# A talking-heads attention and SoLU kernel: new due times in its planner, v in six pieces, a longer ring, another tile order

## Chip, cores and metric

The kernel runs on one core of one Trainium2 chip (trn2). The metric is the device time in microseconds (us) of one execution; three executions of the kernel before gave a median of 728.68 us.

## What is computed

Four batches, 12 heads, 448 positions, 64 values per head; then 1792 tokens (4 x 448) of width 768 through a SoLU layer with 1024 hidden units. All inputs and the output are float32 in their values. Shortened from the reference:

```python
scores = np.matmul(q, k.transpose(0, 1, 3, 2)) / np.sqrt(64)     # q, k, v: (4, 12, 448, 64)
scores = np.einsum('bhij,hg->bgij', scores, w_pre)               # heads mixed before softmax
attn = np.exp(scores - np.max(scores, axis=-1, keepdims=True))
attn = attn / (np.sum(attn, axis=-1, keepdims=True) + 1e-09)
attn = np.einsum('bhij,hg->bgij', attn, w_post)                  # and after it
x = np.matmul(attn, v).transpose(0, 2, 1, 3).reshape(1792, 768)
h = x @ w_in                                                     # 768 x 1024
e = np.exp(h - np.max(h, axis=-1, keepdims=True))
solu = h * e / (np.sum(e, axis=-1, keepdims=True) + 1e-09)
mu = np.mean(solu, axis=-1, keepdims=True)
var = np.mean((solu - mu) ** 2, axis=-1, keepdims=True)
out = ((solu - mu) / np.sqrt(var + 1e-06) * g_ln) @ w_out        # 1024 x 768
```

## The kernel before

Every matmul whose operands are split runs as three float16 products (high x high, high x low, low x high). The attention part walks through the batches b = 0 to 3. Each batch has 45 units u of 10 query rows (the last unit of a batch has 8), gathered in four blocks of 12 or 9 units (120 or 88 rows). Two units make a pair, and one pair passes through these steps, each a task of the planner:

- `qk` (L502, PE), once for two heads and a block: the scores of the block, into PSUM; `sh` (L514, ACT) and `sl` (L519, DVE) write them as high and low halves into a tile `s`, of which there are two.
- `f` (L553, L557, a DMA issued on SP): it gathers 10 rows of all heads from `s` into `sr`, of which there are four.
- `m` (L570, PE): mixing with w_pre. `mx` (L580, DVE) row maximum, `ex` (L596, ACT) exponential with its sum, `gd` and `iv` (L607, L611, DVE) reciprocal of the sum, `w` (L617, POOL) the weights of w_post divided by the sum, `o` (L625, PE) mixing with w_post, `po` (L251 through `copy`, ACT) into the ring `p_t`, 18 units long.
- once per block `av` (L675, PE), six calls of two heads each, then `xh` (L242, ACT) and `xl` (L247, DVE), which write x into `x_t` in two groups of three calls. They share one PSUM bank.

While batch b - 1 runs, q, k and v of batch b are prepared: loads `ld` (issued on POOL), absolute maxima `am` (L405 on DVE for q and k, L403 on ACT for v), a short chain of scales `sc`, the halves `hi` (L244, POOL) and `lo` (L247 on DVE or L437 and L438 on POOL), and DMA transposes `t` (issued on SP). v lies in a pool of two whole tiles of 12 heads, loaded by six transfers; its maxima are taken in four pieces of 768 columns. In the last batch w_in takes the place of the next batch: `fw` (fetch), `wi` (steps that turn 64-bit floats into 32-bit ones), `wm` (L800, maximum), `wh` and `wl` (halves); then `h0`, the hidden matmuls of the first token tile. The x of batches 0 to 2 is stored to DRAM (`xd`), and `x0` loads batch 0's back during the last batch.

The order of all this is fixed when the program is made, by the class `Plan`: a list scheduler with a cost for each task. It keeps for each engine the time at which it is free and takes, again and again, an engine's best task: of those that could start within `LOOK` us of the earliest, the one with the smallest sum of its due time and `RUSH` times its extra wait. With `RUSH = 12.0` and `LOOK = 0.25` that is nearly the one that is ready first; due times come from `at`, `T0 + STEP * (45 b + u)` with T0 = 24 and STEP = 2.25 us. A transfer counts as landed 2.2 us (2.6 us from POOL) plus its bytes after its issue. `ring`, `until` and `more` say how many buffers a tile has and which tasks free them. On the chip each engine then runs its own queue in that order and waits on semaphores.

After the attention part its pools are closed and the SoLU part (`moe`) begins, in plain program order: two pieces of w_out are fetched (`cv_wo`), then x of batches 1 and 2 (`x_fetch`, L729 and L731, on SP). A loop over t then runs `solu_mean(t)`, from t = 11 on `project(t - 11)` (L1397, PE), `hidden(t + 1)` (L838, PE), `solu_head(t + 1)`, `ln(t)`, for t below 8 a conversion of one piece of w_out (L757 to L776), and the DMA transposes `turn`. Tile t is 128 tokens. Pools that are opened here lie on the addresses of those that were closed, so that a first transfer into them waits for the old tile's last reader.

## Time and profile before

| | us |
|---|---|
| median of 3 runs | 728.68 (726.76 to 728.98) |
| the profiled execution | 729.22 |
| its span, first to last instruction | 727.5 |
| PE busy | 642.6 (88%) |
| DVE busy | 506.5 (70%) |
| ACT busy | 454.8 (63%) |
| POOL busy | 271.1 (37%) |
| mean granted clock of PE | 0.97 |

Shares of the whole span mix three parts: a start of some 50 us, the attention part until 492.7 us, when the last x is written, and the SoLU part. They have to be read by stretches: for each stretch the time in which PE did nothing, the clock that it was granted (1.00 is 2.4 GHz, 0.50 is 1.2 GHz), and which other engine was busy nearly all the time. The profiled execution lies 0.5 us above the median of the runs.

### The profile page before, as it was taken

What the parts mean: (1) busy time and instruction counts of PE and PEld (TensorE: products, weight loads), DVE (VectorE), ACT (ScalarE), POOL (GpSimd) and SP (SyncE); (2) the same over time, 40 slices, a digit from 0 to 9 for tenths busy, and PEclk for the clock granted to TensorE, in tenths of its full rate; (3) what the DMA queues carried; (4) which work ended last, traced back from release to release, by engine and by line L of the source; (5) the groups of instructions that cost most, each with busy time, mean ns of one, the idle gap of its engine ahead of it and who ended that gap; (6) DMA issues with size and microseconds to landing.
All of it is one profiled execution on the core that took longest, in us unless ns stands there. A gap on an engine that the chain in (4) does not pass through costs nothing.

```text
span 727.5 us, 17255 instructions
## 1 busy us (share of the span) xinstructions
PE 642.6 (88%) x6418; PEld 427.1 (59%) x6418; DVE 506.5 (70%) x1345; ACT 454.8 (63%) x960; POOL 271.1 (37%) x418
## 2 busy tenths in 40 slices
PE   2677979999899899889998988979998848999997
PEld 2444757777667577667776766754443424566664
DVE  7875998879997569997779999748888764200000
ACT  2655778887688778769798876724555554321111
POOL 3503584124961124871113443502666633320000
PEclk9698999999999999999999998999999979999999
DMA  8037479355678547598266545226367313244112
GB/s 228 14 74 202 128 195 184 126 171 170 201 188 167 126 115 219 189 209 205 79 216 199 198 171 166 59 88 194 91 132 170 59 29 52 51 102 93 44 44 66
DMA packets 114028, 98.51 MB, mean 135 GB/s; under 512 B 69604, under 2 KB 104600, under 8 KB 113944
## 3 DMA queue, kind: packets, MB, share of 16 engines
q1 hardware_dynamic: 108120, 83.62, 43.7%
q0 software_dynamic: 4416, 12.40, 5.9%
q10 hardware_dynamic: 1408, 1.38, 0.7%
q8 instruction: 51, 0.84, 0.5%
q14 instruction: 33, 0.27, 0.1%
HBM read 33.24 MB, written 9.63 MB: 59 GB/s over the span
## 4 chain that ended last, share of the span: by engine, by line
PE 46%; DVE 30%; DMA 8%; ACT 6%; POOL 5%; issue 3%; SPq 1%; ACTq 0%; POOLq 0%; DVEq 0%
PE y L1397 14%; PE po L625 13%; PE px L675 6%; DVE dead L580 5%; PE pm L570 5%; PE ps L502 5%; DVE s L519 4%; DMA sr<-s 4%; PE ps_h L838 3%; POOL wo L776 2%; DVE cv_wo L773 2%; ACT e L596 2%; DVE hl_q L247 2%; DMA raw_q<-in_q_dram 2%; DVE cv_wo L768 1%
## 5 line engine op out<-in xcount | busy, mean ns | idle before, releaser
L625 PE MATMUL po<-wr,e 128*112 128x120 f32 x1440 | 179.3, 278 | 19.6 <-POOL wr L617 19.4
L625 PEld LDWEIGHTS po<-wr,e 128*112 128x112 f32 x1440 | 160.0, 182 | 48.2 <-POOL wr L617 34.7
L617 POOL TENSOR_SCALAR wr<-wq,sm 128x120 f32<-128x120 f32 x180 | 72.9, 415 | 259.2 <-DVE sm L611 92.2
L596 ACT ACTIVATE e<-pm,nb,c_exp 128x448 f32<-128x448 f32 x180 | 132.9, 738 | 31.6 <-DVE dead L580 28.4
L580 DVE TENSOR_SCALAR_CACHE_REDUCE dead<-pm,c_nexp 128x448 f16<-128x448 f32 x180 | 121.8, 677 | 24.4 <-PE pm L570 16.0
L514 ACT ACTIVATE s<-ps 120x448 f16<-120x448 f32 (+1 forms) x192 | 100.1, 549 | 51.8 <-PE ps L502 39.7
L519 DVE SCALAR_TENSOR_TENSOR s<-ps,s 120x448 f16<-120x448 f32 (+1 forms) x192 | 115.5, 617 | 21.6 <-ACT s L514 16.8
L251 ACT COPY p_t<-po 112x480 f32<-112x480 f32 x180 | 109.9, 626 | 16.8 <-PE po L625 16.1
L675 PE MATMUL px<-p_t,raw_v 112*64 112x120 f32 (+1 forms) x1536 | 90.0, 264 | 5.6 <-ACT p_t L251 2.3
L502 PE MATMUL ps<-k,q 64*64 64x448 f16 (+2 forms) x1008 | 82.7, 362 | 11.5 <-DVE s L519 7.1
L838 PE MATMUL ps_h<-wi,xf 128*128 128x512 f16 x396 | 86.8, 379 | 5.7 <-DVE u L1340 5.7
L675 PEld LDWEIGHTS px<-p_t,raw_v 112*64 112x64 f32 x1536 | 74.1, 136 | 26.5 <-issue 15.0
L1397 PE MATMUL y<-wo_h,lth 128*128 128x384 f16 (+2 forms) x224 | 72.7, 331 | 9.8 <-ACT wo_h L242 9.8
L1397 PE MATMUL y<-wo_l,lth 128*128 128x384 f16 (+2 forms) x224 | 72.4, 329 | 2.5 <-DVE wo_l L247 2.0
L1397 PE MATMUL y<-wo_h,ltl 128*128 128x384 f16 (+2 forms) x224 | 72.4, 330 | 0.0
L1397 PEld LDWEIGHTS <-lth 128*128 128x128 f16 x448 | 44.3, 99 | 43.8 <-issue 15.4
L838 PEld LDWEIGHTS <-xf 128*128 128x128 f16 x396 | 38.5, 98 | 52.8 <-issue 7.4
L570 PE MATMUL pm<-sr,wp_hi 64*64 64x448 f16 (+1 forms) x720 | 58.0, 367 | 9.3 <-DMA sr<-s 6.0
L1405 ACT ACTIVATE o<-y,c_out 128x384 f32<-128x384 f32 (+2 forms) x28 | 16.1, 578 | 72.3 <-PE y L1397 72.3
L502 PEld LDWEIGHTS <-q 64*64 64x64 f16 (+2 forms) x1008 | 33.8, 108 | 40.9 <-issue 21.0
L596 ACT ACTIVATION_READ_ACCUMULATOR e<-pm,nb,c_exp 128x1 f32 x180 | 38.4, 213 | 0.0
L570 PE MATMUL pm<-sr,wp_lo 64*64 64x448 f16 (+1 forms) x360 | 36.5, 355 | 0.0
(178 smaller groups left out, 798.8 us busy)
## 6 DMA issues: line engine op xcount, KB each, us to landing
sr<-s SPq DMA_DIRECT2D x176, 210.0 KB
cv_wi<-in_moe_w_in_dram SPq DMA_DIRECT2D x24, 256.0 KB
cv_wo<-in_moe_w_out_dram SPq DMA_DIRECT2D x8, 768.0 KB
raw_k<-in_k_dram POOLq DMA_DIRECT2D x18, 224.0 KB, 4.0
raw_q<-in_q_dram POOLq DMA_DIRECT2D x18, 224.0 KB, 5.6
raw_v<-in_v_dram POOLq DMA_DIRECT2D x18, 224.0 KB, 4.5
xh<-xsh SPq DMA_DIRECT2D x9, 224.0 KB
xl<-xsl SPq DMA_DIRECT2D x9, 224.0 KB
```

The lines of the kernel that those rows point to most:

```text
L251: nc.scalar.copy(out=out, in_=in_)
L502: nc.tensor.matmul(sps[b, c, h + e][lo:hi], q2[b, g][rows, 2 * j + x, i0 + lo : i0 + hi], k1[b, g][rows, 2 * j + y], start=(a == 0), stop= ...
L514: nc.scalar.activation(out=s_t[b, c][0 : y.shape[0], h, 0], in_=y, func=AF.Copy, scale=2.0**-E_S)
L519: nc.vector.scalar_tensor_tensor(out=t[:, h, 1], in0=y, scalar=2.0**-E_S, in1=t[:, h, 0], op0=ALU.mult, op1=ALU.subtract)
L570: nc.tensor.matmul(pmx[b, u + i][64 * e : 64 * e + 64, 0:S], w[rows], sr[b, u][rows, e, z], start=(a == 0), stop=(a == 2),)
L580: nc.vector.tensor_scalar(out=dead, in0=pmx[b, u][:, 0:S], scalar1=c_nexp[0:UK, b : b + 1], scalar2=None, op0=ALU.mult, op1=ALU.min, accum ...
L596: nc.scalar.activation(out=ee[b, u], in_=pmx.pop((b, u))[:, 0:S], func=AF.Exp, bias=nbs.pop((b, u)), scale=c_exp[0:UK, b : b + 1], accum_o ...
L617: ENG[eng].tensor_scalar(out=w, in0=wq[0:UK, 0 : H * UN], scalar1=sm, scalar2=1.0, op0=ALU.mult, op1=ALU.mult)
L625: nc.tensor.matmul(ps[:, c * 120 : (c + 1) * 120], e[:, c * CP : (c + 1) * CP], w, start=True, stop=True)
L675: nc.tensor.matmul(xps[b, blk, g][e * 64 : e * 64 + 64, i, 0:n], raws["v", b][:, h, c * D : (c + 1) * D], block_view(b, blk, c * H + h), s ...
L838: nc.tensor.matmul(ps[:, n], xx[:, kc, o : o + 128], ww[:, kc, n * 512 : (n + 1) * 512], start=(kc == 0 and a == 0), stop=(kc == KDM - 1 a ...
L1397: nc.tensor.matmul(y, xx[:, kc], ww[:, kc, cut], start=(kc == 0 and a == 0), stop=(kc == KFF - 1 and a == 2),)
```

## The change

The planner: `LAG` adds a time by the kind of the transfer to the planned landing (fetch `f` 1 us, `ld` 4.24, `t` 3, `xd` 7.9, `fw` 10). `RUSH` falls from 12.0 to 0.04 and `LOOK` to 0.143, so that of the tasks that are ready within 0.143 us the one due first is taken, nearly whatever it waits. Due times are rewritten: pairs replace units as their clock, 4.2 us for a pair (`PER`), and `AIM` adds an offset to each kind of task, from -182 (`t` of k) to +258 us (`lo` of q); such offsets are ranks more than times. `ld` of k and q become due from the batch's start (`ago(0.6 * i)`), with the same dependence on the `m` of the batch before.

v: its pool has seven tiles of two heads; a piece of the next batch needs the slot that `av` of the last block frees for the same heads. Its maxima are taken in six pieces of 512 columns, each after its own load. The ring `p_t` has 24 units instead of 18, and starts at 15 instead of 9.

SoLU: tiles are taken in the order 11, 12, 13, 0, ..., 10. `x0` is gone; x of batch 0 is fetched with the others after the attention part. `h0` waits for the `xl` of the last batch's first two blocks instead. `wm` may run on ACT. `av` of batch 0 waits for the warming matmuls.

```diff
-    RUSH = 12.0
-    LOOK = 0.25
+    RUSH = 0.04
+    LOOK = 0.143
+    AIM = {
+        "am_k": 211, "am_q": 63, "am_v": 143, "av0": 53, "av1": 46, "av2": 15, "av3": 21, "av4": 63,
+        "av5": -125, "es": 199, "ex0": -9, "ex1": 38, "f0": -126, "f1": -104, "gd0": -94, "h0": 123,
+        "iv0": -15, "ld_v": 45, "lo_k": 140, "lo_q": 258, "lo_q0": 233, "m0": -20, "mix": -100, "mx0": 17,
+        "mx1": 17, "o0": 11, "po0": -10, "qk": -17, "sc_k": -53, "sc_q": -51, "sc_wi": -44, "sh0": -33,
+        "sh1": -168, "sl1": 12, "t_k": -182, "t_q0": -144, "wh": 82, "wi": 93, "wl": 45, "xh0": -26,
+        "xh1": -59, "xl0": -166,
+    }
+    LAG = {
+        "f": 1, "fw": 10, "ld": 4.24, "t": 3, "xd": 7.9,
+    }
...
+        tasks = {k: t[:3] + (t[3] + self.aim(k),) + t[4:] for k, t in self.tasks.items()}
...
+                lag = (2.6 if e == "pool" else 2.2) + self.LAG.get(k[0], 0.0)
...
-                    rings[i] = max(rings[i], t + (2.6 if e == "pool" else 2.2)) + kb / ways / rate
+                    rings[i] = max(rings[i], t + lag) + kb / ways / rate
...
-    T0, STEP = 24, 2.25
-    RING = 18
+    T0, PER = 24, 4.2
+    RING, NV = 24, 7
...
-    v_p = ctx.enter_context(tc.tile_pool(name="vp", bufs=2))
+    v_p = st.enter_context(tc.tile_pool(name="vp", bufs=NV))
...
-        return (RING // 2 + b * NU + u) % RING * UN
+        return (15 + b * NU + u) % RING * UN
...
-        assert n == 2 * m
-        (pp, np), (ce, _) = x.ap
-        return bass.AP(x.tensor, x.offset + i * ce, [[pp, np], [-i * ce, 2], [ce, m]])
+        if n == 2 * m:
+            (pp, np), (ce, _) = x.ap
+            return [(slice(0, n), bass.AP(x.tensor, x.offset + i * ce, [[pp, np], [-i * ce, 2], [ce, m]]))]
+        views = [(slice(0, m), x[:, i : i + m])]
+        return views + ([(slice(m, n), x[:, 0 : n - m])] if m < n else [])
...
-        for i in (i,):
+        for cut in [cut for cut, _ in block_views(b, blk, 0)]:
             for c in range(NCH):
                 for e in range(2):
...
-                        due=at(b - 1, 6 + i) if b else i + 4 * (n == "q"),
+                        due=ago(0.6 * i + 3 * (n == "q")) if b else i + 4 * (n == "q"),
...
-                    after=[("m", b - 1, 14 + 2 * i)] if b else [("am", "q", 0, 1)],
+                    after=[("m", b - 1, 40)] if b else [("am", "q", 0, 1)],
...
-                    until=[("av", b, NBLK[b] - 1, NPAIR - 1)],
+                    until=[("av", b, NBLK[b] - 1, i)],
...
-                    AMV,
+                    {"act": (0.61, 0.71)},
...
-                    after=[("lo", "q", o, NPAIR - 1), ("m", o, i + 4 * kc)],
+                    after=[("lo", "q", o, NPAIR - 1)],
...
-            add(("wm", kc), with_eng(w_in_max, kc), {"dve": 1.13}, after=[prev], due=due + 9)
+            add(("wm", kc), with_eng(w_in_max, kc), {"dve": 1.13, "act": (1.0, 1.1)}, after=[prev], due=due + 12)
...
+    T3 = -(-(B - 1) * S // 128)
+    TURNS = list(range(T3, NT)) + list(range(T3))
...
-        for b, pool, tag in ((1, v_p, "v"), (2, wt_p, "x2")):
+        for b in range(B - 1):
             for i in range(XP):
-                x_fetch(b, i, pool, tag)
+                x_fetch(b, i, wt_p)
```

## Rows read from the trace of the kernel before

**Rows 1.** The page: busy time of PE, and the chain that ended last, by engine

```profile
PE 642.6 (88%) x6418; PEld 427.1 (59%) x6418; DVE 506.5 (70%) x1345; ACT 454.8 (63%) x960; POOL 271.1 (37%) x418
PE 46%; DVE 30%; DMA 8%; ACT 6%; POOL 5%; issue 3%; SPq 1%; ACTq 0%; POOLq 0%; DVEq 0%
```

**Rows 2.** Windows: stretch, its length, busy us by engine, granted clock, DMA share, GB/s

```profile
52.00:72.00 20.00, 13.96 (x133) 8.87 (x133) 11.38 (x33) 11.85 (x29) 6.75 (x13) 0.87 0.70 196
84.00:110.00 26.00, 21.34 (x291) 15.99 (x288) 24.78 (x76) 20.32 (x49) 21.51 (x38) 1.00 0.53 148
110.00:180.00 70.00, 67.56 (x921) 52.05 (x921) 57.95 (x171) 60.26 (x141) 22.70 (x50) 1.00 0.58 158
180.00:220.00 40.00, 35.70 (x439) 26.07 (x437) 37.94 (x111) 31.80 (x73) 30.86 (x55) 1.00 0.71 201
240.00:258.00 18.00, 15.08 (x161) 9.79 (x160) 10.45 (x32) 12.88 (x31) 2.13 (x6) 0.91 0.49 119
286.00:321.00 35.00, 30.38 (x395) 22.41 (x391) 33.36 (x97) 25.81 (x62) 26.81 (x46) 0.95 0.75 210
386.00:452.00 66.00, 57.72 (x702) 41.74 (x695) 64.21 (x147) 53.03 (x116) 26.51 (x33) 0.98 0.59 194
452.00:492.70 40.70, 36.16 (x384) 27.00 (x383) 24.76 (x61) 19.32 (x41) 11.98 (x15) 0.95 0.27 80
492.70:574.90 82.20, 76.46 (x354) 34.30 (x351) 71.57 (x150) 43.31 (x66) 49.28 (x31) 1.00 0.59 136
606.70:727.50 120.80, 117.12 (x698) 68.01 (x695) 10.44 (x32) 26.12 (x42) 14.74 (x11) 1.00 0.30 68
```

**Rows 3.** Chain that ended last, in order of time, near the first batch's start

```profile
56.39 10.51 DMA sr<-s
```

**Rows 4.** Timeline of POOL: first loads of the next batch's k (twelve of k, q)

```profile
54.53 2.04 POOL L393 DMA_DIRECT2D raw_k<-in_k_dram  x3
```

**Rows 5.** Groups by line: count, busy us, mean ns; preparation of q, k, w_in on DVE

```profile
L405 DVE TENSOR_REDUCE am_q<-raw_q 112x1 f32<-112x768 f32 x16 | 15.1, 943 | 1.8 <-DMA raw_q<-in_q_dram 1.8
L247 DVE SCALAR_TENSOR_TENSOR hl_q<-raw_q,p_q,hl_q 112x256 f16<-112x256 f32 x34 | 20.5, 648 | 0.0
L800 DVE TENSOR_REDUCE am_wi<-wi 128x1 f32<-128x1024 f32 x6 | 7.3, 1210 | 0.4 <-POOL wi L776 0.4
```

**Rows 6.** Groups by line: ACT's maxima of v, and its pass over 512 columns

```profile
L403 ACT ACTIVATE ja_v<-raw_v 112x768 f16<-112x768 f32 x16 | 13.9, 871 | 0.0
L242 ACT ACTIVATE hl_q<-raw_q,p_q 112x512 f16<-112x512 f32 x6 | 3.9, 711 | 0.0
L403 ACT ACTIVATION_READ_ACCUMULATOR ja_v<-raw_v 112x1 f32 x16 | 3.6, 225 | 0.0
```

**Rows 7.** Chain that ended last: the low halves of w_in

```profile
469.38 7.63 DVE wi L247 x5
```

**Rows 8.** Groups by line and form, 484 to 492 us: `av` of the last block

```profile
L675 PE MATMUL px<-p_t,raw_v 112*64 112x88 f32 x96 | 4.1, 241 | 2.3 <-DVE xsl L247 1.7 <-ACT p_t L251 0.6
L675 PEld LDWEIGHTS px<-p_t,raw_v 112*64 112x64 f32 x96 | 3.8, 137 | 2.6 <-issue 1.9 <-ACT p_t L251 0.8
```

**Rows 9.** Timeline of SP's queue: fetches of w_out and x

```profile
484.78 0.82 SPq L742 DMA_DIRECT2D cv_wo<-in_moe_w_out_dram  x2
491.12 1.47 SPq L729 DMA_DIRECT2D xf<-xh  x3
501.70 0.60 SPq L731 DMA_DIRECT2D xf<-xsl  x1
505.66 10.01 SPq L742 DMA_DIRECT2D cv_wo<-in_moe_w_out_dram  x2
```

**Rows 10.** The page's DMA issues: count and KB of each piece of x of batch 0

```profile
xf<-xh SPq DMA_DIRECT2D x3, 256.0 KB
```

**Rows 11.** Window with the fetches at full share, and DVE's timeline

```profile
496.00:498.00 2.00, 2.00 (x11) 0.94 (x10) 0.64 (x4) 1.43 (x3) 0.00 (x0) 1.00 1.00 300
511.27 0.55 DVE L757 TENSOR_SCALAR cv_wo<-cv_wo 128x768 uint32<-128x768 uint32 x1
```

More of the change, by code (lines that the diff above doesn't have):

```diff
@@ L39, in add, with aim @@
         self.tasks[key] = (run, on, list(after), due, ring, slots, dma, list(behind), shape)
+    def aim(self, k):
+        if not isinstance(k, tuple):
+            return self.AIM.get("misc", 0.0)
+        n = k[0]
+        if n in ("m", "mx", "ex", "w", "o", "po", "f", "gd", "iv"):
+            n += str(int("pe" not in self.tasks[("m",) + k[1:]][1]))
+        elif n in ("sh", "sl"):
+            n += str(k[3] % 2) + ("p" if k[1] == 0 and k[2] == 0 else "")
+        elif n in ("av", "xh", "xl"):
+            n += str(k[3])
+        elif n in ("hi", "lo", "am", "ld", "t", "tp"):
+            n += "_" + k[1] + ("0" if n == "tp" or k[2] == 0 else "")
+        elif n == "sc":
+            n += "_" + str(k[1])
+        return self.AIM.get(n, 0.0)
     def order(self):
-        tasks, done, out = self.tasks, {}, []
+        done, out = {}, []
+        tasks = {k: t[:3] + (t[3] + self.aim(k),) + t[4:] for k, t in self.tasks.items()}
         held = {r: [] for r in self.size}
@@ L849, in add_tasks, with pt, at @@
         with_eng = lambda f, *a: lambda e: f(*a, e)
-        at = lambda b, u: T0 + STEP * (b * NU + u)
-        none = ()
+        pairs, first = [], {}
+        for b in range(B):
+            for c in range(NBLK[b]):
+                first[b, c] = len(pairs)
+                pairs += [(b, u) for u in range(BLK0[b][c], BLK0[b][c + 1], 2)]
+            first[b, NBLK[b]] = len(pairs)
+        clock = [T0]
+        for b, u in pairs:
+            clock.append(clock[-1] + PER * (1.0 if pair_of(b, u)[1] == 2 else 0.6))
+        when = {g: t for g, t in zip(pairs, clock)}
+        def pt(i):
+            if i != int(i):
+                return pt(i // 1) + PER * (i % 1)
+            i = int(i)
+            if i < 0:
+                return T0 + PER * i
+            return clock[i] if i < len(clock) else clock[-1] + PER * (i - len(clock) + 1)
+        def at(b, u):
+            if u >= NU:
+                return at(b + 1, u - NU) if b + 1 < B else pt(len(pairs)) + PER / 2 * (u - NU)
+            if u < 0 or b < 0:
+                return at(b - 1, u + NU) if b > 0 else T0 + PER / 2 * (b * NU + u)
+            u0, _ = pair_of(b, u)
+            return when[b, u0] + PER / 2 * (u - u0)
         add("mixl", mix_load, {"pool": (2.3, 9.3)}, due=0.0)
@@ L949, in add_tasks @@
                     )
-            add(("es", b), one(exp_scales, b), {"dve": 0.28}, after=es, due=at(b - 1, 35) if b else T0 - -2)
+            add(("es", b), one(exp_scales, b), {"dve": 0.28}, after=es, due=ago(20) if b else T0 - -2)
             for i in range(NPAIR):
@@ L1140, in add_tasks @@
         o = B - 1
-        for i in range(XP):
-            add(
-                ("x0", i),
-                one(x_fetch, 0, i, v_p, "v"),
-                {"sp": 0.57},
-                dma=(16, 229, 18.5),
-                after=[("xd", b, j) for b in range(2) for j in range(XP)] + [("m", o, 28 + 2 * i)],
-                behind=[("x0", i - 1)] if i else [],
-                due=at(o, 30 + 2 * i),
-                ring=None if i else "v",
-                until=["end"],
-            )
         for kc in range(KDM):
-            due = at(o, 18 + 4 * kc)
+            due = pt(first[o, 0] - 3 + 3.2 * kc)
             for i in range(4):
@@ L1193, in add_tasks @@
             )
-            add(("wl", kc), with_eng(w_in_lo, kc), {"dve": 1.19}, after=[("wh", kc)], due=at(o, 33 + 2 * kc))
+            add(("wl", kc), with_eng(w_in_lo, kc), {"dve": 1.19}, after=[("wh", kc)], due=pt(first[o, 0] + 18.5 + 0.8 * kc))
         prev = []
```

141 lines of the change are left out of this document (73 added, 68 removed).

## The prediction, made before the changed kernel was run

> **What bounds the kernel now.** I read the page first, then windows by stage, then inside each weak stage the chain and the timelines. The page says that PE is busy 88% of the span and carries 46% of the chain that ended last, DVE 30% [rows 1]. Such shares mix stages, so the windows come next [rows 2]. In the middle of a batch (110 to 180 us) PE works 67.56 of 70 us: it is the bound there, and 3.5% idle is what the present planner reaches when nothing disturbs. The weak stretches are others, and their idle PE time is the length less the busy time in [rows 2]: 6.0 us in 52 to 72; 4.7 in 84 to 110, 4.3 in 180 to 220 and 4.6 in 286 to 321; 2.9 in 240 to 258; 8.3 in 386 to 452; 4.5 in 452 to 492.7. Together 35.4 us. In five of these the granted clock, 2.4 GHz at 1.00, was also below that, part of the time at 1.2 GHz, in stretches in which PE had idled; the length times the missing share times PE's busy share is what that cost: 1.8, 1.5 (286 to 321), 1.4 (240 to 258), 1.1 and 1.8 us, 7.6 in all. Had these 245.7 us only 3.5% of idle time, 8.6 us would stay. So everything that a better order can win before 492.7 us is 35.4 + 7.6 - 8.6 = 34.4 us.
>
> Behind 492.7 us the loop of the SoLU part is led by DVE (71.57 of 82.2 us), then PE works 117.12 of 120.8 us [rows 2]. The change leaves the work of both as it is; that part moves with the time at which it begins. The time before 52 us I count at nothing: the loads and scales of batch 0 are the same.
>
> **Part by part: due times, RUSH, LOOK, AIM.** These remove no instruction; they change which of two ready tasks is issued first. Before, ready first was issued first, so preparation ran when its data came. The three stretches at 84, 180 and 286 us show it: DVE is busy 24.78 of 26, 37.94 of 40 and 33.36 of 35 us there, but only 57.95 of 70 in 110 to 180 [rows 2]. What fills it is the next batch's maxima and low halves, 0.943 and 0.648 us each (16 and 34 of q, about as many of k) [rows 5], and the softmax of the current pair stands behind them. With offsets of +63 to +258 these become filler for idle moments. The room is there (12 us in 110 to 180), the need is some 18 us for a batch: 8 maxima of 0.943 and about 14 low halves of 0.648, as batch 0 takes 24 of the 66, and scales. The three stretches hold 13.6 us idle and 1.5 of clock, less 3.5% of 101 us: 11.6. I take 60%, 7.0 us, because most of the need fits the room; bounds 0 and 11.6.
>
> The last batch is the same case with w_in: DVE is busy 64.21 of 66 us in 386 to 452 [rows 2]. `fw` no longer waits for a unit of the last batch, and `wm`, 6 of 1.21 us [rows 5], may run on ACT, which has 13 us to spare there. Open: 8.3 + 1.1 - 2.3 = 7.1 us; I take 60%, 4.3. Behind it five low halves of w_in hold DVE for 7.63 us [rows 7] while the last pairs wait. Open in 452 to 492.7: 4.5 + 1.8 - 1.4 = 4.9; I take 40%, 2.0, since all w_in must still be done before `h0`.
>
> **LAG.** It makes no transfer shorter. At the first batch's start one gather into `sr` is in the chain for 10.51 us [rows 3]; POOL had begun to issue the twelve loads of the next k and q at 54.53 us [rows 4], and the sixteen engines moved 196 GB/s in the stretch [rows 2]. Those loads hang on the same `m` as before, so the crowd comes again; the planner can only put other work, a `qk`, ahead of the premix. Open: 6.0 + 1.8 - 0.7 = 7.1; I take a quarter, 1.8. At 240 to 258 it is the transposes and a gather; `t` of k now goes first on SP. Open: 2.9 + 1.4 - 0.6 = 3.7; half, 1.8.
>
> The Trainium skill says the same against this part (DMA: Bandwidth & Descriptors, "Issuing engines are not separate DMA queues"): DMAs from any engine run on the same 16 DMA engines and interleave. The 10.51 us agree, and by that rule alone the 1.8 us would be nothing.
>
> Gain: 7.0 + 4.3 + 2.0 + 1.8 + 1.8 = 16.9 us, with 0 and 34.4 as bounds.
>
> **v in six pieces.** ACT's maxima become 24 of (0.711 + 0.225) us instead of 16 of (0.871 + 0.225) [rows 6]: 22.5 against 17.5 us, 5.0 more. They hide in ACT's idle time, some 10 us of 70 even in the best stretch [rows 2]; without it they would cost 5.0. The loads are as many, but now wait for the slot that `av` of the last block frees, some 5 pairs into the batch. If they are late, POOL stands at the load, and behind it on POOL `w`, and on PE `o`. The first block's `av` needs them only when its own 9 or 12 units are done, and 24 units of ring are more than two blocks; I count nothing.
>
> **Ring of 24.** Starting at 15 + 45b, only one block wraps at a point that isn't its middle: the last block of the last batch starts at (15 + 135 + 36) mod 24 = 18 with 88 rows, 60 before the end and 28 after. Its matmuls become 96 for each group of three calls. Nothing hides them, as the SoLU loop waits for that x. Now 96 matmuls take 4.1 us and their loads 3.8, so 39.6 ns a load [rows 8]. If the loads set the pace, a group takes 96 x 39.6 ns = 3.8 instead of 2.04 us, 1.76 more, 3.5 for both. If time goes by columns, it is 0. The row's loads were themselves paced by matmuls of 42.5 ns, so I take 1.0 a group: 2.0 us.
>
> The Trainium skill (TensorE: Matmul & The Clock Gate, "LDWEIGHTS") gives columns / 1.2 ns, so an estimate of 53 ns for 64 columns; one after the other, 96 would take 5.1 us and both groups lose 6.2. The row's 39.6 ns show that two overlap, so the measurement decides.
>
> **Tile order.** PE's work is the same. Tiles 12 and 13 need no fetch. But `x0` leaves the last batch, and six transfers of 256 KB [rows 10] join the fetches behind it. SP issued eighteen between 491.12 and 502.3 us and the third piece of w_out at 505.66 [rows 9]; six more at half a microsecond still end by 505.7, so it is the bytes that count. DVE takes that piece at 511.27 us [rows 11], 5.6 us after its issue, and its own 786 KB (128 x 768 values of 8 bytes) need 2.6 us at the 300 GB/s of a full window [rows 11]: 3.0 us to spare. The six bring 1.57 MB, 5.2 us at that rate. And the tiles of w_out may now lie on the ring's addresses, so that their first fetches, issued at 484.78 us [rows 9], would wait for `av` until 491.1; the later of them adds 2.6 us there. Queued ahead in full, DVE's loop stands 5.2 + 2.6 - 3.0 = 4.8 us; at best 0. I take 1.0, since the eighteen (2.7 MB by their shapes) filled only 240 of the 300 GB/s over their 11.2 us and leave room for 0.7 MB.
>
> **Sum.** -16.9 + 2.0 + 1.0 = -13.9 us. The profiled execution took 729.22 us, 1.7 of it around its span of 727.5; 729.2 - 13.9 = 715.3 us. The median of the runs lies 0.5 below that execution, so 714.8.
>
> **Rivals.**
> First, the preparation starves. This is the case on the slower side. With ranks of +140 to +258, `am` and `lo` run only when nothing else is ready. The point from which it decides: if less than the 18 us of a batch's need fits into DVE's idle moments before the boundary, the rest stands before `t` and `qk` of the next batch with PE empty. About 13 us fit by [rows 2] (12 in 110 to 180, 1 in 84 to 110), so 5, and with late data 10 us, stay at each of three boundaries. These take the place of 4.5 us idle now: 3 x 5.5 = 16.5, plus 3.0 of costs: 748 us. Against it: units overlap over the boundary, and 220 to 240 and 258 to 286 gave room as well.
> Second, transfers stay the limit. The bursts at 52 and 240 us don't shrink, and w_in is as late as before because its tiles come free no earlier. Then only the three stretches win: 728.7 - 7.0 + 3.0 = 724.7 us.
> Third, the order doesn't do what it says: waits on the chip differ from the planned ones, idle time only moves to other tasks, and the costs remain: 727 to 733 us.
> Fourth, it does all it can: two thirds to nine tenths of the 34.4 us, less 3: 700.7 to 708.7.
>
> **How the numbers follow.** My forecast (709 to 721 us) 0.42; the fourth case and better 0.22; the second (721 to 726.5) 0.14; the third 0.11, about two thirds of it within 0.3% of 728.7; the first 0.11. A measurement of this kernel can tell some 0.3%, 2.2 us, from no change. Faster: 0.42 + 0.22 + 0.13 = 0.77; same 0.09; slower 0.14. The range of 8 in 10 goes from 698 (below it 0.07: the upper bound of the gain and no cost is 694) to 732 (above it 0.13).
>
> **What would show it.** Right: the stretches at a batch's change keep PE idle under 6%, DVE's load is level over a batch, maxima and low halves are scattered; the last x is written near 478 us, and from there to the end it takes some 235 us as before, plus 1. Wrong: a run of `lo` with PE empty before each boundary (first rival); gathers of 10 us again (second); waits of PE as long as before at other lines (third); DVE idle before L757 in the third turn of the SoLU loop (the fetch term); the last block's groups longer or shorter than 3 us (the ring term).

## The result and the profile after

The changed kernel took 722.77 us (median of 4 runs, 721.44 to 723.45) against 728.83 us of the kernel before beside it on the same chip: a ratio of 0.9919, with a 95% interval of 0.9894 to 0.9944. It is faster by some 6 us where 13.9 were forecast. The profiled execution took 722.47 us, its span 720.8; before these were 729.22 and 727.5, so the two profiles differ by 6.75 us.

The page of the changed kernel, busy time by engine and the chain that ended last [rows 1]:

```profile
PE 651.8 (90%) x6514; PEld 430.3 (60%) x6514; DVE 500.4 (69%) x1331; ACT 455.2 (63%) x977; POOL 282.7 (39%) x447
PE 49%; DVE 26%; DMA 8%; ACT 6%; issue 5%; POOL 4%; SPq 2%; POOLq 0%; DVEq 0%; ACTq 0%
```

The last x of the attention tells the two halves of the kernel apart. DVE's timelines have its last piece here, in the kernel before and in the changed one:

```profile
491.79 0.87 DVE L247 SCALAR_TENSOR_TENSOR xsl<-px,x_sc,xsh 128x80 f16<-128x80 f32 x4 [2.89 <-ACT xsh L242]
476.52 0.87 DVE L276 SCALAR_TENSOR_TENSOR xsl<-px,x_sc,xsh 128x80 f16<-128x80 f32 x4 [3.89 <-ACT xsh L271]
```

It ends at 492.66 us before and at 477.39 after: the attention won 15.3 us (forecast: -16.9 + 2.0 = -14.9). From there to the end of the span it took 243.4 us, before 234.8: the SoLU part lost 8.6 us (forecast: 1.0). Gain and loss make the 6.7 us. So the question is where the 8.6 us came from, and whether the 15.3 were won for the reasons that I gave.

**The attention by stage**, the windows of [rows 2], in the changed kernel (the first row, 20 to 52 us, is new):

```profile
20.00:52.00 32.00, 25.86 (x246) 15.44 (x243) 27.81 (x66) 20.40 (x45) 12.05 (x19) 0.89 0.23 58
52.00:72.00 20.00, 16.26 (x192) 11.01 (x189) 14.52 (x38) 14.59 (x33) 9.14 (x18) 1.00 0.72 194
84.00:110.00 26.00, 24.31 (x286) 17.64 (x286) 25.49 (x72) 21.68 (x51) 21.57 (x41) 1.00 0.62 167
110.00:180.00 70.00, 69.64 (x914) 52.25 (x916) 59.08 (x171) 62.33 (x148) 29.23 (x61) 1.00 0.62 183
180.00:220.00 40.00, 35.70 (x426) 26.43 (x424) 34.11 (x102) 30.44 (x73) 22.30 (x40) 1.00 0.78 175
240.00:258.00 18.00, 17.92 (x231) 13.09 (x233) 14.29 (x41) 16.57 (x39) 7.36 (x15) 1.00 0.58 155
286.00:321.00 35.00, 30.23 (x384) 23.13 (x382) 30.81 (x98) 28.21 (x71) 22.61 (x43) 0.95 0.93 209
386.00:452.00 66.00, 60.03 (x698) 44.97 (x690) 59.52 (x147) 53.70 (x119) 27.81 (x34) 0.97 0.44 138
```

and the kernel before in that first stretch:

```profile
20.00:52.00 32.00, 22.43 (x218) 13.98 (x216) 25.77 (x61) 18.50 (x37) 8.63 (x18) 0.79 0.16 38
```

PE is busier by 3.4 us in 20 to 52, 2.3 in 52 to 72, 3.0 in 84 to 110, 2.1 in 110 to 180, 2.8 in 240 to 258 and 2.3 in 386 to 452, and no busier in 180 to 220 and 286 to 321. From the second batch on the windows no longer hold the same work, since the changed kernel runs ahead. ACT's copies into `p_t` show by how much. There are 180, 45 for each batch; the 45th, 90th, 135th and 180th end at about 160, 271, 373 and 485 us before and at 152, 251, 363 and 468 after, so 9, 20, 10 and 17 us ahead.

**The SoLU part.** Its loop is followed by the start of each product `u` (L1340 before, L1401 after), counted from the last x, in us:

```
turn              0     1     2     3     4     5     6     7     8     9     10     11     12    end of span
before         6.55 14.91 24.66 34.39 44.13 53.88 63.62 73.36 80.81 87.32 102.23 114.03 125.08  234.84
after          7.73 16.07 29.32 39.40 49.47 59.53 69.60 79.67 86.24 92.74 107.67 119.47 133.07  243.41
later by       1.18  1.16  4.66  5.01  5.34  5.65  5.98  6.31  5.43  5.42   5.44   5.44   7.99    8.57
```

Four steps are seen: 1.2 us before the first turn, 3.5 in turn 2, some 0.33 in each of the five turns behind it (10.07 us instead of 9.74; 0.9 of it comes back in turn 8), and 2.55 between turns 11 and 12. SP's timeline shows what stands ahead of turn 2:

```profile
475.95 0.81 SPq L775 DMA_DIRECT2D cv_wo<-in_moe_w_out_dram  x2
477.48 3.74 SPq L762 DMA_DIRECT2D xf<-xh  x3
481.27 2.73 SPq L762 DMA_DIRECT2D xf<-xl  x3
495.17 0.61 SPq L764 DMA_DIRECT2D xf<-xsl  x1
495.88 9.85 SPq L775 DMA_DIRECT2D cv_wo<-in_moe_w_out_dram  x2
```

The 24 transfers of x are issued from 477.48 to 495.8 us: 18.3 us, and up to 1.78 us for one. The third piece of w_out goes out behind them at 495.88, though ACT's maximum, which reads its buffer last, was done at 491.5:

```profile
491.29 0.19 ACT L1351 ACTIVATION_READ_ACCUMULATOR cv_wo<-wo 128x1 f32 x1
```

In DVE's timeline the piece is taken with a wait of 4.08 us (the next ones with half a microsecond to one, and a longer instruction; their rows are in the last section):

```profile
501.32 0.56 DVE L790 TENSOR_SCALAR cv_wo<-cv_wo 128x768 uint32<-128x768 uint32 x1 [4.08 <-DMA cv_wo<-in_moe_w_out_dram]
```

The chain that ended last goes through a fetch in each of these turns, which it did in none before:

```profile
495.88 5.34 DMA cv_wo<-in_moe_w_out_dram
505.38 4.64 DMA cv_wo<-in_moe_w_out_dram
515.46 5.11 DMA cv_wo<-in_moe_w_out_dram
```

### The profile page after: what moved, and what is told of

It is laid out like the page before. It is cut to its first block, busy times and chain, and to the rows that moved or that the text cites. A ratio compares the mean times of both kernels' runs of the same rounds, so it can differ in the third digit from the quotient of the medians.

```text
span 720.8 us, 17481 instructions
## 1 busy us (share of the span) xinstructions
PE 651.8 (90%) x6514; PEld 430.3 (60%) x6514; DVE 500.4 (69%) x1331; ACT 455.2 (63%) x977; POOL 282.7 (39%) x447
## 4 chain that ended last, share of the span: by engine, by line
PE 49%; DVE 26%; DMA 8%; ACT 6%; issue 5%; POOL 4%; SPq 2%; POOLq 0%; DVEq 0%; ACTq 0%
PE y L1458 15%; PE po L659 14%; PE px L708 6%; PE pm L604 5%; PE ps L534 5%; DVE dead L614 5%; DVE s L551 4%; DMA cv_wo<-in_moe_w_out_dram 4%; PE ps_h L876 3%; DMA sr<-s 2%; ACT e L630 2%; DVE hl_k L276 2%; DVE sm L641 2%; DVE hl_q L276 1%; DVE u L1387 1%
## 5 line engine op out<-in xcount | busy, mean ns | idle before, releaser
L659 PE MATMUL po<-wr,e 128*112 128x120 f32 x1440 | 184.6, 279 | 15.3 <-POOL wr L651 12.3
L651 POOL TENSOR_SCALAR wr<-wq,sm 128x120 f32<-128x120 f32 x180 | 70.8, 403 | 217.4 <-DVE sm L645 124.7
L551 DVE SCALAR_TENSOR_TENSOR s<-ps,s 120x448 f16<-120x448 f32 (+1 forms) x192 | 112.4, 616 | 19.0 <-ACT s L546 17.5
L546 ACT ACTIVATE s<-ps 120x448 f16<-120x448 f32 (+1 forms) x192 | 93.9, 546 | 23.7 <-PE ps L534 20.4
L876 PE MATMUL ps_h<-wi,xf 128*128 128x512 f16 x396 | 91.2, 392 | 6.5 <-DVE u L1401 6.5
L708 PE MATMUL px<-p_t,raw_v 112*64 112x120 f32 (+3 forms) x1632 | 88.2, 259 | 1.9 <-ACT e L630 0.8
L708 PEld LDWEIGHTS px<-p_t,raw_v 112*64 112x64 f32 x1632 | 76.0, 137 | 15.5 <-issue 9.3
L534 PE MATMUL ps<-k,q 64*64 64x448 f16 (+2 forms) x1008 | 79.5, 356 | 5.1 <-DVE s L551 3.3
L876 PEld LDWEIGHTS <-xf 128*128 128x128 f16 x396 | 40.0, 101 | 56.9 <-issue 13.8
L604 PE MATMUL pm<-sr,wp_hi 64*64 64x448 f16 x720 | 58.3, 362 | 5.6 <-DMA sr<-s 3.5
L534 PEld LDWEIGHTS <-q 64*64 64x64 f16 (+2 forms) x1008 | 31.9, 106 | 31.6 <-issue 15.3
L1432 POOL TENSOR_TENSOR ll<-u,lh 128x1024 f16<-128x1024 f32 x14 | 30.4, 2171 | 19.2 <-ACT lh L1430 19.2
```

The lines of the kernel that those rows point to most:

```text
L534: nc.tensor.matmul(sps[b, c, h + e][lo:hi], q2[b, g][rows, 2 * j + x, i0 + lo : i0 + hi], k1[b, g][rows, 2 * j + y], start=(a == 0), stop= ...
L546: nc.scalar.activation(out=s_t[b, c][0 : y.shape[0], h, 0], in_=y, func=AF.Copy, scale=2.0**-E_S)
L551: nc.vector.scalar_tensor_tensor(out=t[:, h, 1], in0=y, scalar=2.0**-E_S, in1=t[:, h, 0], op0=ALU.mult, op1=ALU.subtract)
L604: nc.tensor.matmul(pmx[b, u + i][64 * e : 64 * e + 64, 0:S], w[rows], sr[b, u][rows, e, z], start=(a == 0), stop=(a == 2),)
L651: ENG[eng].tensor_scalar(out=w, in0=wq[0:UK, 0 : H * UN], scalar1=sm, scalar2=1.0, op0=ALU.mult, op1=ALU.mult)
L659: nc.tensor.matmul(ps[:, c * 120 : (c + 1) * 120], e[:, c * CP : (c + 1) * CP], w, start=True, stop=True)
```

## Experiments on the SoLU part

The theory after the result: fetches of w_out stand in SP's queue behind transfers that nobody needs yet. The rival is the one of my own prediction, that bytes count and not issues. Ratios are to the kernel before on the same chip (the changed kernel itself: 0.9919).

**x fetched later.** The x of batches 1 and 2 is fetched inside the loop, behind the w_out fetches of turns 1 and 3.

```
-        for b in range(B - 1):
-            for i in range(XP):
-                x_fetch(b, i, wt_p)
+        for i in range(XP):
+            x_fetch(0, i, wt_p)
 ...
                 fetch_w_out(t + 2)
+            if t in (1, 3):
+                for i in range(XP):
+                    x_fetch((t + 1) // 2, i, wt_p)
```

> The changed kernel, but x of batches 1 and 2 is fetched inside the SoLU loop, behind the w_out pieces of its turns 1 and 3; only x of batch 0 stays ahead of it. Theory: in the changed kernel SP was still issuing x when the buffer for the third piece of w_out came free, and the late piece put the loop into a longer turn (10.07 us instead of 9.74). Then the part from the last x to the end falls from 243.4 to 236 to 237 us, DVE's wait of 4.08 us before its third L790 goes, and the time is 716 to 717 us. Rival: the loop is slower by the new tile order or the new addresses themselves; then the part stays at 243 and the time at 722.8.

Measured: 718.20 us, 0.9849 (0.9805 to 0.9892); the SoLU part is 240.7 us, less than the 243.4 of the changed kernel but not the 236 to 237 expected. Turn 2 begins without a wait, and four turns take 9.70 to 9.77 us. Then the twelve issues of batch 2 at 523 to 531 us, with two transposes behind them, hold the next w_out fetch back until 534.27, and the same stall comes at that place, in DVE's timeline:

```profile
540.02 0.90 DVE L790 TENSOR_SCALAR cv_wo<-cv_wo 128x768 uint32<-128x768 uint32 x1 [3.32 <-DMA cv_wo<-in_moe_w_out_dram]
```

The stall has moved to behind the twelve issues of batch 2, and a turn of 10.07 us follows it. The six issues of batch 1, at 503.6 to 506.6 us, cost nothing that shows.

**Issue or bytes.** The changed kernel, with the w_out pieces from the third on issued on ACT's queue right behind the maximum that frees their buffer. The x transfers, their bytes and their place stay.

```
                 nc.scalar.activation(out=ex, in_=t, func=AF.Abs, accum_out=am_o[:, kc : kc + 1])
+                if kc + 2 < KFF:
+                    fetch_w_out(kc + 2, nc.scalar)
 ...
-            if t + 2 < KFF:
-                fetch_w_out(t + 2)
```

> The changed kernel; only the w_out pieces from the third on are issued on ACT's queue, right behind the maximum that frees their buffer, and no longer on SP's behind the x transfers and the transposes. My prediction held that issue is cheap and that bytes count. If the bytes of the x transfers are what made the third piece late, it still lands about when it did: DVE waits 3 to 4 us for it as in the changed kernel (4.1), and the total stays at 721 to 724 us. If SP's queue is (24 issues stretched over 18.3 us, the fetch behind them), the fetch goes out some 4.4 us earlier and the wait falls to 1 us or less; the total falls by 3 to 5 us, to 717 to 720.

Measured: 716.78 us, 0.9835 (0.9776 to 0.9894). ACT's timeline has the issue at 490.63 us, DVE's the piece without a wait, 5.66 us later:

```profile
490.63 0.36 ACTq L775 DMA_DIRECT2D cv_wo<-in_moe_w_out_dram  x1
```

```profile
496.29 0.55 DVE L790 TENSOR_SCALAR cv_wo<-cv_wo 128x768 uint32<-128x768 uint32 x1
```

The window between them shows that the x transfers ran at full rate beside it (DMA share 0.94, 298 GB/s):

```profile
491.00:496.00 5.00, 5.00 (x25) 2.23 (x23) 4.96 (x7) 2.29 (x3) 3.38 (x2) 1.00 0.94 298
```

The turns from 1 to 6 take 9.74 us each. The same x bytes at the same full rate no longer delay the pieces behind them, so the rival falls: it was the place in SP's queue. The Trainium skill (DMA: Bandwidth & Descriptors, "Issuing engines are not separate DMA queues") says that starting DMAs on several engines at once saves only the sequencer's time for starting them, which it calls usually small beside the transfer itself. Here that time was, in the changed kernel, 4.4 us of waiting behind other issues, on the path, and the measurement decides.

Of the 6 us that the run gains over the changed kernel its profile shows 3.2 behind the last x (a SoLU part of 240.1 us). The last x comes 1.9 us earlier too, at 475.46, and the edit does not explain that; in two other profiles with this order it comes at 476.2 and 477.9. What stays of the 8.6 us: 2.2 ahead of turn 0, as the first piece is still late, and the 2.5 before turn 12.

**Tile order alone.** The kernel before, with the old planner, in which only the tile order and the x fetches are those of the change (no `x0` in the last batch; six more transfers behind it; v's pool closed with the attention).

```
-            for i in range(XP):
-                x_fetch(b, i, pool, tag)
+        for b in range(B - 1):
+            for i in range(XP):
+                x_fetch(b, i, wt_p)
 ...
+        t = TURNS[t]
+        if t >= T3:
+            return x_t[B - 1][0], x_t[B - 1][1], t * 128 - (B - 1) * S
```

> The kernel before with the new tile order alone: x of batch 0 is fetched after the attention part, v's pool is closed with it, tiles run 11, 12, 13, 0 to 10; planner, v and ring as before. Theory: the loss behind the last x belongs to this part of the change: from the last x to the end 241 to 244 us instead of 234.8, time 735 to 738 us. Rival: the loss comes from the new addresses behind the longer ring alone; then 235 to 236 us behind the last x, 729 to 730 us. If the x of batch 0 had disturbed the last batch, its part would become shorter.

Measured: 730.39 us, 1.0029 (1.0005 to 1.0053). The last x comes 3.0 us earlier (489.63), as `x0` no longer stands in the last batch, and the SoLU part is 4.2 us longer (239.1). DVE waits 1.08 us for the third piece, and then the long turns of 10.05 to 10.09 us are there:

```profile
509.99 1.27 DVE L757 TENSOR_SCALAR cv_wo<-cv_wo 128x768 uint32<-128x768 uint32 x1 [1.08 <-DMA cv_wo<-in_moe_w_out_dram]
519.66 1.68 DVE L757 TENSOR_SCALAR cv_wo<-cv_wo 128x768 uint32<-128x768 uint32 x1 [0.66 <-DMA cv_wo<-in_moe_w_out_dram]
```

So the stall and the long turns come with the tile order and its fetches, under the old planner too. But this is 4.2 of the 8.6 us, where the theory expected 6 to 9. The rows show a second cause beside it. SP's timeline of this run has

```profile
481.77 0.80 SPq L742 DMA_DIRECT2D cv_wo<-in_moe_w_out_dram  x2
505.43 0.55 SPq L742 DMA_DIRECT2D cv_wo<-in_moe_w_out_dram  x1
```

The first two pieces of w_out go out 7.9 us ahead of the last x, as in the kernel before. In the changed kernel they go out 1.4 us ahead of it, at 475.95, since in its chain they stand behind the last group of `av`:

```profile
472.89 2.94 PE px L708 x96
475.83 0.02 SPq L775
```

The x transfers follow right behind them there. With 24 of these in both, the third piece leaves 15.8 us behind the last x here and 18.5 us in the changed kernel, and DVE waits 1.08 and 4.08 us for it. So the larger part of that wait goes with the late first pieces and not with the six transfers alone. The two kernels differ in the planner, too; an edit that moves w_out's buffers in the changed kernel follows below.

**The low clock before turn 12.** In the windows of the changed kernel the granted clock is 0.50, so 1.2 GHz, behind a stretch in which PE worked 0.58 of 3 us. In the kernel before it stays at 1.00, so 2.4 GHz, behind the same place, where PE worked 0.41 of 3 us. First the changed kernel, then the one before:

```profile
591.00:594.00 3.00, 0.58 (x4) 0.22 (x3) 1.12 (x3) 1.97 (x3) 0.42 (x1) 0.94 0.00 0
594.00:597.00 3.00, 2.55 (x8) 1.11 (x8) 2.72 (x8) 0.97 (x2) 0.26 (x1) 0.50 0.00 0
597.00:600.00 3.00, 3.00 (x10) 1.21 (x8) 1.30 (x3) 2.02 (x3) 1.84 (x2) 0.50 0.26 52
```

```profile
601.00:604.00 3.00, 0.41 (x3) 0.12 (x2) 0.96 (x3) 2.14 (x4) 0.26 (x1) 1.00 0.00 0
604.00:607.00 3.00, 2.40 (x14) 1.32 (x14) 2.88 (x8) 0.81 (x1) 0.42 (x1) 1.00 0.00 0
```

PE stands there for 2.62 us, until ACT has the seventh piece of `wo_h`, in both kernels. To tell the wait from the change, the 36 hidden matmuls of the next tile, which PE takes behind this projection, were put between its sixth and seventh piece, in the changed kernel and in the one before.

```
                 for kc in range(KFF):
+                    if kc == 6 and mid:
+                        mid()
 ...
-                project(t - LAG)
+                project(t - LAG, (lambda: hidden(t + 1)) if t == LAG else None)
 ...
-                hidden(t + 1)
+                if t != LAG:
+                    hidden(t + 1)
```

> The changed kernel; in the first output projection, PE takes the 36 hidden matmuls of the twelfth step between the sixth and the seventh piece of w_out instead of behind the eighth, so that it no longer stands 2.62 us for the last pieces. If the low granted clock (0.50 at 594 to 600 us) comes from that stand, the step from the eleventh to the twelfth u, 13.6 us in the changed kernel, becomes 10.5 to 11.1 us at a clock of 1.00, and the total falls by 2.5 to 5 us, to 718 to 720. If the clock falls for another reason, it is 0.50 again near that place, and the gain is at most the stand itself, 0 to 2.6 us.

> The kernel before with the same move of the 36 hidden matmuls. Its profile had the same stand of 2.62 us, but a clock of 1.00 behind it. If that was chance and most of its executions have the low clock, as the profiles of other kernels with the same stand do, it gains 2.5 to 5 us like the changed kernel, 724 to 726 us beside 728. If the low clock belongs to the change, it gains 2.6 us at most.

Measured: 716.45 us, 0.9858 (0.9815 to 0.9901) for the changed kernel, and 723.69 us, 0.9954 (0.9932 to 0.9977) for the one before. PE's timeline of the first shows the matmuls without a wait ahead of them, 7.93 us long (8.97 in the changed kernel); the granted clock is 1.00 from 588 us on:

```profile
590.49 7.93 PE L876 MATMUL ps_h<-wi,xf 128*128 128x512 f16 x36
```

From the start of turn 11 to that of turn 13 both now take 23.76 us, instead of 29.16 in the changed kernel and 26.61 in the one before: 5.4 and 2.85 us less. So 2.85 us are the wait, which both have, and the other 2.55 are the clock, which fell in the profile of the changed kernel and not in that of the one before. Of the 14 profiles without this move the clock is low at this place, in part or in full, in 12, with the old planner too; the step from turn 11 to 12 took 12.18 to 13.60 us there and 11.0 in the other two. It goes with the wait, not with a line of the change.

So the 2.55 us are a difference of two profiles. By the medians the move gains about as much in both kernels: the ratio of the two with it is 0.9904 (0.9858 / 0.9954), without it 0.9919. That the clock costs the changed kernel more than the one before is not shown by the runs.

**All remedies.** The changed kernel with the x of batch 1 in turn 1 and that of batch 2 in turn 6, behind the last w_out fetch; with w_out's buffers laid ahead of the pool of x, so that the first two pieces no longer wait for the attention; and with a ring offset of 21, which puts the uneven wrap into batch 0. An earlier form of it had batch 2 in turn 3.

```
+            if t in (1, 6):
+                for i in range(XP):
+                    x_fetch(1 if t == 1 else 2, i, wt_p)
 ...
-        wt_p = ctx.enter_context(tc.tile_pool(name="wt", bufs=1))
         h_p = ctx.enter_context(tc.tile_pool(name="hp", bufs=2))
         cv_p = ctx.enter_context(tc.tile_pool(name="cv", bufs=2))
+        wt_p = ctx.enter_context(tc.tile_pool(name="wt", bufs=1))
 ...
-        return (15 + b * NU + u) % RING * UN
+        return (21 + b * NU + u) % RING * UN
```

> The changed kernel with three edits: x of batches 1 and 2 inside the SoLU loop (as x_late), the ring started at 21 (as ring_21), and the pool of the w_out pieces laid ahead of the weights' pool, on addresses that q, k and s leave before the ring does. Theory: the three losses behind the attention part were separate, 6 to 7 us at the third piece, 1.9 at the last block, 1.2 at the first piece; together 712 to 714 us. Rival: one of them hides behind another; 715 to 718 us.

> The changed kernel with the x of batch 1 fetched in turn 1 of the loop and that of batch 2 in turn 6, behind the last fetch of w_out, with w_out's buffers laid where their first fetches need not wait for the attention's last block, and with a ring offset of 21, so that the uneven wrap falls in batch 0. No fetch of w_out is then queued behind x transfers. If the fetch term explains the SoLU part's added 8.6 us but for the clock, all turns take 9.7 us, DVE never waits for w_out, and the SoLU part is 235 to 237.5 us; total 711 to 715 us. If not, turns of over 10 us stay and the SoLU part is over 238 us.

> The kernel with x spread over turns 1 and 6 and offset 21, and besides w_out's later pieces issued on ACT's queue. If SP's queue still delays a fetch (transposes ahead of it), this gains another 0.5 to 2 us over the run with SP; if with spread x every fetch is early enough, both are the same within 1 us, as the turn is then set by DVE's and POOL's work alone.

> The kernel with x spread over turns 1 and 6, w_out's buffers laid apart and offset 21, and with the same move of the 36 hidden matmuls. That kernel's profile had no low clock at this place (step of 11.04 us). It should gain the stand of 2.6 us, and in the executions in which the clock would have fallen 2 us more: 711 to 713.5 us. A time above 714 would say that the stand cost nothing, or that the stall moves to the next wait.

Measured: with batch 2 in turn 3 716.80 us, 0.9834 (0.9791 to 0.9876), not the 712 to 714 expected, again with a wait (0.48 us) and two long turns behind its twelve issues. In turn 6 715.64 us, 0.9830 (0.9781 to 0.9878): DVE never waits for w_out, the turns from 1 to 6 take 9.73 to 9.75 us, and the SoLU part is 235.7 us, that of the kernel before with 0.8 us on top. Neither its profile nor that of the kernel before has the low clock ahead of turn 12. What the moved buffers bring is seen in turn 0: it begins 6.7 us behind the last x, in the kernel before 6.55, in the changed kernel 7.73, and 9.19 in the run in which x alone was fetched later. The w_out fetches on ACT's queue add nothing to that: 716.35 us, 0.9830 (0.9779 to 0.9881). With the 36 matmuls moved too it is 710.77 us, 0.9777 (0.9743 to 0.9811), the fastest here: 2.2% below the kernel before.

## Experiments on the attention part

**Offsets and choice.** The changed kernel with an empty `AIM`, and with `AIM` but the old `RUSH` and `LOOK`.

```
-    AIM = {
-        "am_k": 211, "am_q": 63, ...
-    }
+    AIM = {}
```

> The changed kernel with an empty AIM: the due times as written, no offsets; RUSH, LOOK, LAG, due formulas, v in six pieces and the ring stay. If the searched offsets bring the attention part its 15.3 us (my three-stretches and w_in terms went by them), the last x comes 8 us or more later than 477.4 us, at 485 to 493, and the total is 730 us or more. If the rewritten due times, the v slots and the lag do the work, the last x stays within 4 us of 477.4 and the total is 719 to 727.

```
-    RUSH = 0.04
-    LOOK = 0.143
+    RUSH = 12.0
+    LOOK = 0.25
```

> The changed kernel with the old way of choosing (RUSH 12, LOOK 0.25), the offsets kept. If the offsets work only because the rule now lets a due time decide, the last x comes 8 us or more later than 477.4 us and the total is over 730 us, as with no offsets at all. If the offsets alone do it, the last x stays within 4 us and the total is 720 to 727 us. In both cases the SoLU part stays at 242 to 244 us from the last x.

Measured: 744.14 us, 1.0208 (1.0148 to 1.0268) without offsets, 737.14 us, 1.0125 (1.0080 to 1.0171) with the old choice. The last x comes at 505.3 and 492.3 us, 28 and 15 us later than in the changed kernel (the first of these profiles, of an execution of 749.58 us, lies 5.4 us above its median). Both are needed for the gain: the new due times and the new rule without offsets are 12.7 us behind the kernel before, and the offsets under the old rule are level with it. That does not make each worthless by itself, since the lag table stays in both runs, and with the old order alone it costs 19.6 us, as the next run shows. PE's timeline without offsets shows one place among others, the last block: each of its groups waits for DVE.

```profile
496.07 2.99 PE L701 MATMUL px<-p_t,raw_v 112*64 112x60 f32 x96 [1.63 <-DVE xsl L269]
500.77 2.99 PE L701 MATMUL px<-p_t,raw_v 112*64 112x60 f32 x96 [1.72 <-DVE xsl L269]
```

**The lag.** The kernel before with the lag table alone, and the changed kernel without the lag on the loads of q, k and v.

```
+    LAG = {"f": 1, "fw": 10, "ld": 4.24, "t": 3, "xd": 7.9}
 ...
+                lag = (2.6 if e == "pool" else 2.2) + self.LAG.get(k[0], 0.0)
```

> The kernel before with the lag table alone: the planner counts the landings of ld, t, f, fw and xd later by those figures, and nothing else is changed. My terms gave the lag 1.8 us at 52 to 72 us and 1.8 us at 240 to 258. If that is right on its own, the last x comes at 488 to 491 us instead of 492.7 and the total falls by 2 to 4 us, to 725 to 727 beside 728.8. The rival, that a lag without new ranks moves waits and wins nothing: 728 to 733 us.

```
-        "f": 1, "fw": 10, "ld": 4.24, "t": 3, "xd": 7.9,
+        "f": 1, "fw": 10, "ld": 0.0, "t": 3, "xd": 7.9
```

> The changed kernel with no lag on the loads of q, k and v (4.24 us to 0), the other lags kept. If the lag on loads is what made the first gather of batch 0 short (10.51 us before, about 7 us after), a wait of 10 us comes back in the chain at 52 to 72 us and the last x is 3 to 6 us later than 477.4; total 725 to 729. If the ranks do it, the last x stays within 3 us and the total at 720 to 726.

Measured: the lag alone 750.75 us, 1.0321 (1.0285 to 1.0358), 3% slower and outside both expectations; without the lag on loads 722.60 us, 0.9936 (0.9913 to 0.9959), as the changed kernel, with the last x at 477.9. On its own, the lag makes the old order worse. The last x comes at 512.2 us, 19.6 later than in the kernel before. Of this 6.0 are lost by the 135th copy into `p_t`, so most of it in the last batch. Its PE timeline has a long run of the first tile's hidden matmuls ahead of the last pair (14 of them, 3.19 us, at that place in the kernel before); what that cost was not tried:

```profile
494.27 9.19 PE L840 MATMUL ps_h<-wi,xf 128*128 128x512 f16 x34 [1.39 <-DVE wi L249]
503.29 0.98 PE L627 MATMUL po<-wr,e 128*112 128x120 f32 x8
504.84 2.04 PE L677 MATMUL px<-p_t,raw_v 112*64 112x88 f32 x48 [0.57 <-ACT p_t L253]
```

What the other lags bring in the changed kernel was not tried.

**The ring.** The changed kernel with offset 21; and the kernel with x in turns 1 and 6 with the change's own 15.

> The changed kernel with the ring started at 21 instead of 15, so that the uneven wrap falls into the first block of batch 0 and the last block of the last batch is whole. Theory: the two groups of av of the last block take 2.04 instead of 2.99 us, on the path that sets the end: 1.9 us less, 720.9 us. Rival: the groups hide behind the hidden matmuls that the planner put between them, 722.8 us.

> The kernel of the run beside it (x fetched in turns 1 and 6, w_out's buffers elsewhere) with the changed kernel's own ring offset of 15. If the uneven wrap of the last block costs 1.9 us at the end of the attention and nothing is gained for it, this is 1 to 3 us slower than with offset 21, 713 to 717 us. If the offset only moves the cost into batch 0, both are within 1 us of each other.

Measured: 722.65 us, 0.9934 (0.9905 to 0.9964), and 717.36 us, 0.9844 (0.9802 to 0.9885). The groups of the last block are 2.04 us each with offset 21 and 2.99 with 15. In the changed kernel nothing is won by it, since the planner, given another ring, finds another order, and the last x comes at 480.9. In the other pair the last x comes 2.0 us earlier with 21 and the time is 1.7 us lower, as expected, but the intervals overlap.

## Why the prediction was half right

**The sum of the attention was right, its places were not.** -15.3 us against -14.9. Of the 7.0 us that I gave to the three stretches at a batch's change, 84 to 110 us brought 3.0; PE is no busier in the other two, and by the copies the gain lies in batches 0, 1 and 3, while batch 2 gave 10 us back. The sign of PE idle under 6% there did not come: it is idle for 6.5, 10.8 and 13.6% of the three windows, and for 4.6, 10.8 and 10.2% when they are moved 10, 10 and 20 us ahead, as the kernel runs ahead. The first 52 us, which I counted at nothing, brought 3.4 us of PE work. DVE is still busy 25.5 of 26 us at the first change: its preparation was not thinned out there, as I had argued, but PE had other work ready. That the sum fits is in part luck. That the gain needs the offsets and the new rule together is shown by the two runs without the one or the other. How they win it, by filling DVE's idle moments or otherwise, is not shown. The first rival, preparation that starves, had its 748 us not in this kernel, but the same planner without offsets came to 744. It was level with the kernel before until early in the last batch (ACT's 160th pass over the scores of 192 ends at 368.5 us against 367.5) and 12 us behind at the last of them (451.5 against 439.5), so it lost beside w_in and not at the boundaries.

**LAG.** I gave it 3.6 us in two places. Near the first batch's start two gathers are in the chain of the changed kernel, 13.8 us together; before there were two as well, the one of [rows 3] and one of 4.71 us ahead of it, 15.2 us together. First the changed kernel, then the one before:

```profile
44.69 6.57 DMA sr<-s
55.31 7.25 DMA sr<-s
```

```profile
44.01 4.71 DMA sr<-s
```

So the chain won 1.4 us in these gathers. PE is 2.3 us busier in 52 to 72 us and 2.8 in 240 to 258, where I had given 1.8 to each, but these windows do not tell the lag from the new order. The lag of the loads does not bring that time: without it the last x is the same within 0.6 us. That a lag alone would gain is refuted.

**v in six pieces.** 24 maxima of 639 + 208 ns, so 20.3 us against 17.5: 2.8 us more, where I had reckoned 5.0. That they are hidden, as forecast, no run shows by itself, since none takes the six pieces away.

**The ring term.** Forecast 1.0 us for each of the two groups, from 2.04 to about 3; PE's timeline of the changed kernel has them at 2.99:

```profile
468.07 2.99 PE L708 MATMUL px<-p_t,raw_v 112*64 112x60 f32 x96
472.82 2.99 PE L708 MATMUL px<-p_t,raw_v 112*64 112x60 f32 x96
```

**The fetch term is the step that failed**: +1.0, with 4.8 as its bound, against +8.6, and with it the sentence that the SoLU part "moves with the time at which it begins". The reasoning at fault is "six more at half a microsecond still end by 505.7, so it is the bytes that count". The two windows of the x fetches, from the first to the last issue before and to the third piece of w_out after, show the difference:

```profile
491.10:502.30 11.20, 11.20 (x53) 5.07 (x54) 8.72 (x32) 4.32 (x8) 0.41 (x1) 1.00 0.81 222
```

```profile
477.50:495.90 18.40, 18.40 (x87) 8.35 (x86) 14.52 (x40) 8.45 (x12) 5.83 (x4) 1.00 1.00 301
```

The eighteen issues before took 11.2 us, with room on the engines (DMA share 0.81), and SP then stood idle for 3.4 us, until ACT's maximum ended at 505.6 and the piece's buffer was free. With two pieces of w_out and 24 transfers in a row the sixteen engines were full (1.00), SP stood at its issues, and the 24 took 18.3 us; they also began 0.1 us behind the last x instead of 1.5 ahead of it. So the third piece left 18.5 us behind the last x instead of 13.0. I had weighed bytes against the landing time and left out that issues can be held up, and with them everything behind them on SP. I had also put the late first pieces at next to nothing, though the bound held them. With the first piece's 1.2, the sum of the stalls is 4.7 us, nearly the whole bound of 4.8. The other 3.9 are terms that I did not have. A late piece does not cost once: each turn's fetch waits for the maximum of the turn, so a turn that begins late fetches late, and five turns stay 0.33 us long (0.9 of these 1.65 come back). And 2.55 us, in this pair of profiles, are the clock behind PE's wait for `wo_h`, which the trace of before did not show, with 0.6 behind it.

The sign was named: "DVE idle before L757 in the third turn of the SoLU loop (the fetch term)". It is what came, 4.08 us at L790 of the changed kernel.

## What to carry to other kernels

When transfers are moved in a queue, count how long its issues themselves take when the engines are full, and look for the next latency-bound fetch behind them on the same issuing engine; a fetch that frees a loop belongs ahead of bulk that is needed later, or on another engine's queue. A loop in which the fetch of a piece waits for the use of an earlier one can lock into a longer turn after a single stall, so a late piece is to be priced by turns and not once. Parameters found by a search belong together: half of the set can be worse than the old one.

## What was not expected of the hardware

**A locked turn.** The long turns hold no more work than the others. In DVE's timeline the instruction that takes a piece, 0.55 us elsewhere, is 1.35 and 1.85 us long, and in POOL's the product of the piece before ends 0.41 to 0.42 us before it does, at 511.55 and 521.61 us:

```profile
510.12 1.85 DVE L790 TENSOR_SCALAR cv_wo<-cv_wo 128x768 uint32<-128x768 uint32 x1 [0.50 <-DMA cv_wo<-in_moe_w_out_dram]
520.67 1.35 DVE L790 TENSOR_SCALAR cv_wo<-cv_wo 128x768 uint32<-128x768 uint32 x1 [0.99 <-DMA cv_wo<-in_moe_w_out_dram]
```

```profile
509.70 1.85 POOL L809 TENSOR_TENSOR wo<-cv_wo 128x768 f32<-128x768 f32 x1 [0.91 <-DVE cv_wo L806]
519.76 1.85 POOL L809 TENSOR_TENSOR wo<-cv_wo 128x768 f32<-128x768 f32 x1 [0.90 <-DVE cv_wo L806]
```

It is as if DVE's instruction got its way only when POOL's was done. The Trainium skill (SBUF — State Buffer, "Who interferes with whom") says that the two share a pair of ports under an exclusive lock, and that of two instructions that use it the one that issues first keeps it and the other blocks; these rows agree. In the short turns DVE's instruction begins just ahead of that product and takes 0.55 us, and it is the product that is longer, 2.10 us instead of 1.85. In the kernel before:

```profile
521.01 0.55 DVE L757 TENSOR_SCALAR cv_wo<-cv_wo 128x768 uint32<-128x768 uint32 x1
521.17 2.10 POOL L776 TENSOR_TENSOR wo<-cv_wo 128x768 f32<-128x768 f32 x1 [0.90 <-DVE cv_wo L773]
```

No run moves the one against the other, so that the lock holds the turn at 10.07 us is argued from these rows.

**A queue that holds back its issuer.** Three of the first six issues of x, right behind the two pieces of w_out, took 1.78, 1.30 and 1.65 us, where most others in this queue take 0.36 to 0.72:

```profile
477.48 1.78 SPq L762
```

Full engines alone do not make them long, since the last twelve took some 0.6 us each, beside a DMA share of 0.87 to 1.10. Nor do the eighteen behind them: in the run with x fetched later only these six stood there, and they took 6.5 us just the same. What does is left open.

**The clock.** A wait of 2.62 us of PE, in a stretch that was thinly used already, was followed by 1.2 GHz in one profile and by 2.4 GHz in another, with the same instructions around it.
